# Fused attention and MLP block: low-part subtractions of the MLP on GpSimd, attention pieces at a higher rate

## The chip, the cores and the metric

The kernel runs on one core of a Trainium2 chip. The core has five engines that run side by side, each with an instruction queue of its own that is worked off in order: TensorE (PE in the profile; its weight loads are listed as PEld), VectorE (DVE), ScalarE (ACT), GpSimd (POOL) and SyncE (SP, which here issues the DMAs). They wait for each other by semaphores. The metric is the device time of one execution in microseconds (us); lower is better.

## The reference, cut to what matters

The input x has 2048 tokens of 576 channels. It is normalized, and the output is the normalized x, plus an attention, plus a token-shift mixer with an MLP behind it, plus x itself:

```python
xn = layernorm(x)
return x + A(xn, wqkv, wo) + B(xn, w1, w2, w3, w4)

# A: 32 heads of 18 channels; each token looks at 8 tokens: itself and those 2, 4, ... 14 before it
logits = q . k[pos - 2*w] * 18**-0.5;  attn = softmax(logits);  o = sum(attn * v[pos - 2*w]);  A = o @ wo
# B: shift mixer, then the MLP of 4608 hidden channels
x1 = xn + shift(gelu(layernorm(xn) @ w1)) @ w2
B = x1 + gelu(layernorm(x1) @ w3) @ w4
```

## The kernel before

Matrix products keep the precision of fp32 by splitting: each operand is the sum of a high part in the type fp32r and a low part, low = operand - high, and a product is hi*hi + hi*lo + lo*hi. So each operand has two steps of preparation: a copy into the high part on ACT (for weights `act.copy`, for the hidden values the gelu itself, once into `hi` and once into an fp32 tile `g`), and a subtraction that gives the low part. `split_w` does both for weights.

The program has stages: a projection to q, k and v (stored in DRAM as `qkvd`), the mixer with w1 and w2, then the MLP with the attention beside it, and last the product with wo. Every engine's order of work is that in which the code issues it; there is no scheduler. What the change touches is the MLP.

The MLP has 72 units (c, b): c counts 18 chunks of two blocks f of 128 hidden channels, b counts four blocks of 512 tokens. In a unit, `up` runs twice (i = 0, 1): 14 matmuls with W3 into a tile p of PSUM (two buffers), two gelus on ACT into `hi` and `g` (`g` has two buffers), and the subtraction that gives `lo` (L682). Then `down` runs four times (j = 0 to 3) for the unit before this one: 12 matmuls with W4 into a tile `ps` of PSUM (three buffers), and DVE adds `ps` to the output sums: Y += ps (L699). `split_w3` and `split_w4` prepare the weights of later blocks, one such split in most units; their raw tiles `rawf` have two buffers, loaded on SP's queue (L177, L173, L505).

The attention has no use of PE apart from the products with wqkv and wo. It is written as a Python generator of small DVE instructions ("pieces"): for each of 8 groups of 4 heads 8 products q*k (L628) and 8 reductions (L631), the scores; a softmax (L636, L641, L643, an exp on ACT, L597, L598, L600); and the weighted sum `av` with 8 products (L608) and 7 additions (L612). The weighted sum of a group comes behind the scores of the next. Loads of q, k, v and the store of the result `od` are issued on SP. In the loop over units, `bg(r)` stands ahead of each `up` and each `down`, six times in a unit, and issues pieces until their estimated cost has used up r:

```python
state["debt"] = min(state["debt"] + us, 1.5)
while state["debt"] > 0 and (late or not state["hold"]):
    cost = next(state["gen"], False)
    ...
    state["debt"] -= cost or 0.0
...
r = RATE[b] / 6 if u >= 4 else 0.0
```

The estimates are 1.3 for a piece of 1152 elements and 0.6 to 0.8 for steps of the softmax. `hold` is set before the exp and lifts only ahead of the down with j = 1. At unit 66 (z = -6) whatever is left of the attention is issued at once, its tiles give way to those of wo, and `load_o` (L738) begins to fetch its output; it is turned by 32x32 transposes on DVE (`turn`, L129 and L130), put to DRAM and fetched back (L137, L142). `split_wo` prepares wo in units 69 to 71; it calls `split_w` with DVE for the subtraction. GpSimd has little to do before the change: inverse square roots for the norms (`pow`, L89), products of one element per partition (L93) and memsets.

Of the kernel before, what the change touches and what calls it, by code (L numbers as in the profile page):

```python
# [8 lines left out]
F32 = mybir.dt.float32  # L9
F32R = mybir.dt.float32r  # L10
AF = mybir.ActivationFunctionType
ALU = mybir.AluOpType
# [33 lines left out]
def fused_block(ctx, tc, x, wqkv, wo, w1, w2, w3, w4, out):  # L46
    nc = tc.nc
    pe, act, dve, pool, sp = nc.tensor, nc.scalar, nc.vector, nc.gpsimd, nc.sync
# [108 lines left out]
    def in_order(blk):  # L157
        return blk.rearrange("p (q t c) -> p t q c", q=4, t=4)

    def by_token(blk):  # L160
        return blk.rearrange("p (t q c) -> p t q c", q=4, t=4)
# [1 line left out]
    def quads(t_, b, q):  # L163
        return dram_ap(t_, (512 * b + 128 * q) * D, [[D, 32], [32 * D, 4], [1, D]])

    def split_w(dst_hi, dst_lo, raw):
        act.copy(dst_hi, raw)  # L167
        dve.tensor_tensor(dst_lo, raw, dst_hi.bitcast(F32), op=ALU.subtract)  # L168

    def dup_tail(dst, w, col, n):  # L170
        ncols = w.shape[1]
# [66 lines left out]
    def split_cg(cg, k0, k1):  # L238
        c, n = COLS[cg]
        split_w(WQ[:, k0:k1, c:c + n], WQ[:, 5 + k0:5 + k1, c:c + n], qraw[cg][:, k0:k1, :])  # L240
# [66 lines left out]
    def split_w1(h):  # L307
        k0, k1 = (0, 3) if h == 0 else (3, 5)
        r = w1raw[h]
        for k in range(k0, k1):  # L310
            src = r[:, (k - k0) * D:(k - k0 + 1) * D].rearrange("p (g c) -> p g c", g=4)
            hi = W1[:, k, 0:512].rearrange("p (g c) -> p g c", g=4)
            lo = W1[:, 5 + k, 0:512].rearrange("p (g c) -> p g c", g=4)
            split_w(hi, lo, src[:, :, :128])
            rem = W1R[:, k, :].rearrange("p (g c) -> p g c", g=4)
            split_w(rem[:, :, 0:16], rem[:, :, 16:32], src[:, :, 128:144])
# [154 lines left out]
    for b in range(NB):  # L471
        for i, m in enumerate((0, 1, 2, 4, 3) if b < 3 else (4, 0, 1, 2, 3)):
# [12 lines left out]
            k = {(0, 4): 0, (1, 1): 1, (1, 4): 2, (2, 1): 3, (2, 4): 4}.get((b, i))  # L485
# [10 lines left out]
    raws, W3, W4 = {}, {}, {}  # L496
# [10 lines left out]
    def split_w3(f):  # L507
        if f >= NF:
            return
        t = W3[f] = wp.tile([128, 10, 128], F32R, name="W3", bufs=3)  # L510
        split_w(t[:, 0:5, :], t[:, 5:10, :], raws[f][:, :640].rearrange("p (k c) -> p k c", k=5))

    def split_w4(f):
        if f >= NF:
            return
        t = W4[f] = wp.tile([128, 2, D], F32R, name="W4", bufs=3)
        split_w(t[:, 0, :], t[:, 1, :], raws[f][:, 640:])

    x1n = {}

# [11 lines left out]
    for t in range(NT):  # L532
        ps = psb.tile([128, 2, 512], F32, name="ps", tag="b")

        def xs(a, t=t):
            if a == 4:
                return T4[:, 2 + t * 128:2 + (t + 1) * 128]
            p, g = divmod(a, 5)
            c = 2 + t * 128 - SHIFT[g]
            return H[p][g][:, c:c + 128]  # L540

        mm_tok(ps, xs, lambda b, h: W2[:, b, h * HF:(h + 1) * HF], HF)
        yv = Y[:, t, :].rearrange("p (h c) -> p h c", h=2)
        dve.tensor_tensor(yv, ps[:, :, :HF], yv, op=ALU.add)
        stats(Y[:, t, :], 2, t)
        if t in (1, 3):
            f = (t - 1) // 2
            split_w3(f)
            split_w4(f)
            load_f(f + 2)  # L550
        if 2 <= t < 6:
            n_turn(t - 2, rzpool)
        if t in (9, 10, 13, 14):
            k = {9: 4, 10: 6, 13: 8, 14: 10}[t]
            n_turn(k, rzpool)
            n_turn(k + 1, rzpool)
        if t in (8, 13):
            x1n[t // 13] = ring_block(("n", t // 13))
            get(("n", t // 13), x1n[t // 13])
        if t in (11, 15):  # L560
            split_x(x1n[t // 15])
# [110 lines left out]
    def up(c, b, i):  # L672
        f = c * C + i
        ps = psa.tile([128, 512], F32, name="p1", tag="a")
        for n, (a, w) in enumerate(PAIRS):
            pe.matmul(ps, W3[f][:, w, :], x1n[b][:, a, :], start=n == 0, stop=n == len(PAIRS) - 1)  # L676
        hi = hp.tile([128, 512], F32R, name=f"hi{i}")
        g32 = hp.tile([128, 512], F32, name="g32")
        lo = hp.tile([128, 512], F32R, name=f"lo{i}")
        act.activation(by_token(hi), in_order(ps), AF.Gelu_apprx_tanh)  # L680
        act.activation(by_token(g32), in_order(ps), AF.Gelu_apprx_tanh)  # L681
        dve.tensor_tensor(lo, g32, hi.bitcast(F32), op=ALU.subtract)  # L682
        hid[c, b, i] = (hi, lo)

    def down(c, b, j):
# [14 lines left out]

    units = [(c, b) for c in range(NCH) for b in range(NB)]
    NU = len(units)
    RATE = [6.1, 6.1, 6.1, 6.1]
    wop = None
    LATE = {(0, 0): (12, 13), (0, 1): (14, 15)}
    Wo = None
# [52 lines left out]
    for u, (c, b) in enumerate(units):  # L759
        if u == 2:  # L760
            ap_pool = apc.__enter__()
            state["gen"] = attention(ap_pool)
            next(state["gen"])
        r = RATE[b] / 6 if u >= 4 else 0.0
        z = u - NU
# [16 lines left out]
        for i in range(C):  # L782
            bg(r, False)
            up(c, b, i)
            if (u, i) in ((0, 0), (1, 0)):
                get(("n", u + 2), x1n[u + 2])
            for t in LATE.get((u, i), ()):
                n_turn(t, tp)
            if u in (1, 2) and i == 0:
                split_x(x1n[u + 1], 0)  # L790
            if z in (-4, -3) and i == 1:
                get(("o", z + 4), o_block(z + 4))
            if z == -2:
                o_turn(2, 2 * i)
                o_turn(2, 2 * i + 1)
            if z == -1:
                split_x(xo[1], i)
        if b == 3:
            split_w3(2 * c + 3)
# [14 lines left out]
        if b == 1:  # L814
            split_w3(2 * c + 2)
        if b == 2:
            split_w4(2 * c + 2)
            load_f(2 * c + 4)
        if b == 0 and c > 0:
            split_w4(2 * c + 1)  # L820
            load_f(2 * c + 3)
# [63 lines left out]
```

## Time and profile before

| | us |
|---|---|
| median of 3 runs (1300.78 to 1302.35) | 1301.79 |
| the profiled execution | 1301.86 |
| its span, first to last instruction | 1300.1 |
| PE busy | 1287.7 |
| DVE busy | 935.5 |
| ACT busy | 361.7 |
| POOL busy | 38.1 |

The MLP with the attention fills the span from about 317 to 1237 us. In the rows of the profile, `128x512` is partitions by elements per partition, a group's row has its count, its busy time, the mean length of one in ns, and the idle time of its engine ahead of it with what ended it. A row of the timeline begins with the start and the length in us. Lengths of instructions that follow each other on one engine overlap a little, so that the step from one start to the next is some 0.08 us shorter than the length. Line numbers are those of the kernel before.

### The profile page before, as it was taken

The numbers are of one execution on the slowest core, as the hardware profiler recorded it, in microseconds if no ns is written. First come the engines' busy times: TensorE is split into PE (matmuls) and PEld (weight loads), VectorE is DVE, ScalarE is ACT, GpSimd is POOL, SyncE is SP. The second block draws the span as 40 slices with busy tenths as digits, with TensorE's granted clock in tenths as the row PEclk, the third lists the DMA queues.
The fourth block names the chain that finished last, engine by engine and source line by source line (L and its number), as shares of the span: only waits on it lengthen the run. The fifth ranks groups of instructions, "written<-read, shape, count | busy, mean of one in ns | idle before, by whom it ended". The sixth has DMA issues, their size and how long they took to land.

```text
span 1300.1 us, 18507 instructions
## 1 busy us (share of the span) xinstructions
PE 1287.7 (99%) x7678; PEld 1186.9 (91%) x7678; DVE 935.5 (72%) x1336; ACT 361.7 (28%) x601; POOL 38.1 (3%) x108
## 2 busy tenths in 40 slices
PE   8999999999999999999999999999999999999898
PEld 8999998899899899999989899999999899999798
DVE  6456535778676778888878888878898877946642
ACT  3322226515422222132232232132232232122300
POOL 2011100021000000000000000000000000000000
PEclk9999999999999999999999999999999999999899
DMA  7646874345602120231221222122222102058542
GB/s 211 155 111 145 172 164 145 102 123 138 214 29 72 40 89 20 81 100 33 68 81 40 81 72 90 44 69 64 66 73 81 43 26 81 20 120 208 154 145 83
DMA packets 157828, 125.20 MB, mean 96 GB/s; under 512 B 72608, under 2 KB 129824, under 8 KB 157744
## 3 DMA queue, kind: packets, MB, share of 16 engines
q1 hardware_dynamic: 157744, 124.02, 34.4%
q8 instruction: 60, 0.98, 0.3%
q14 instruction: 24, 0.20, 0.0%
HBM read 83.56 MB, written 39.39 MB: 95 GB/s over the span
## 4 chain that ended last, share of the span: by engine, by line
PE 93%; DMA 3%; DVE 3%; SPq 1%; ACT 0%; issue 0%; POOL 0%; DVEq 0%
PE ps L696 33%; PE p L676 33%; PE ps L182 18%; PE ps L431 4%; PE ps L276 3%; DMA xd<-st 2%; DVE st L129 1%; DMA xt<-xd 1%; PE ps L446 1%; SPq L137 1%; PE ps L104 0%; DVE Y L699 0%; DMA x1n<-xd 0%; DVE bn L86 0%; PE p L853 0%
## 5 line engine op out<-in xcount | busy, mean ns | idle before, releaser
L696 PE MATMUL ps<-W,hi 128*128 128x288 f32 x2304 | 399.8, 295 | 5.2 <-DVE Y L699 5.2
L696 PEld LDWEIGHTS ps<-W,hi 128*128 128x128 f32 x2304 | 340.3, 188 | 12.1 <-DVE Y L699 5.7
L680 ACT ACTIVATE hi<-p 128x512 fp32r<-128x512 f32 x144 | 86.2, 598 | 576.1 <-PE p L676 576.1
L696 PE MATMUL ps<-W,lo 128*128 128x288 f32 x1152 | 245.8, 295 | 0.0
L676 PE MATMUL p<-x1n,W 128*128 128x512 f32 x1008 | 236.0, 391 | 0.0
L676 PE MATMUL p<-xt,W 128*128 128x512 f32 x1008 | 234.5, 389 | 0.0
L676 PEld LDWEIGHTS p<-x1n,W 128*128 128x128 f32 x1008 | 188.4, 189 | 37.2
L699 DVE TENSOR_TENSOR Y<-ps,Y 128x576 f32<-128x576 f32 x288 | 212.1, 749 | 13.5 <-PE ps L696 13.5
L676 PEld LDWEIGHTS p<-xt,W 128*128 128x128 f32 x1008 | 187.3, 188 | 36.9
L682 DVE TENSOR_TENSOR lo<-g,hi 128x512 fp32r<-128x512 f32 x144 | 99.4, 691 | 158.1 <-ACT g L681 158.0
L696 PEld LDWEIGHTS ps<-W,lo 128*128 128x128 f32 x1152 | 185.9, 188 | 0.0
L182 PE MATMUL ps<-WQ,xt 128*128 128x432 f32 x672 | 134.4, 359 | 0.0
L182 PEld LDWEIGHTS ps<-WQ,xt 128*128 128x128 f32 x672 | 125.5, 188 | 5.4
L628 DVE TENSOR_TENSOR prod<-q,k 128x1152 f32<-128x1152 f32 x64 | 86.4, 1350 | 0.0
L631 DVE TENSOR_REDUCE L<-prod 128x64 f32<-128x1152 f32 x64 | 86.2, 1347 | 0.0
L681 ACT ACTIVATE g<-p 128x512 f32<-128x512 f32 x144 | 85.3, 592 | 0.0
L612 DVE TENSOR_TENSOR o<-o,prod 128x1152 f32<-128x1152 f32 x56 | 75.6, 1350 | 0.0
L608 DVE TENSOR_TENSOR prod<-v,L 128x1152 f32<-128x1152 f32 x56 | 75.6, 1350 | 0.0
L167 ACT CAST W<-rawf 128x640 fp32r<-128x640 f32 x72 | 50.3, 700 | 70.5 <-PE ps L696 69.2
L168 DVE TENSOR_TENSOR W<-rawf,W 128x640 fp32r<-128x640 f32 x72 | 56.3, 785 | 0.0
L182 PE MATMUL ps<-W,h 128*128 128x288 f32 x384 | 53.5, 295 | 0.0
L182 PEld LDWEIGHTS ps<-W,h 128*128 128x128 f32 x384 | 51.9, 188 | 0.1
(108 smaller groups left out, 888.2 us busy)
## 6 DMA issues: line engine op xcount, KB each, us to landing
xd<-st SPq DMA_DIRECT2D x48, 320.0 KB, 6.0
qkvd<-stg SPq DMA_DIRECT2D x24, 432.0 KB, 3.5
rawf<-in_B_w_dram SPq DMA_DIRECT2D x36, 288.0 KB, 3.1
rawf<-in_B_w_dram SPq DMA_DIRECT2D x36, 256.0 KB, 2.9
xt<-xd SPq DMA_DIRECT2D x8, 768.0 KB, 5.1
xin<-in_A_x_dram SPq DMA_DIRECT2D x16, 288.0 KB, 3.8
q<-qkvd SPq DMA_DIRECT2D x8, 576.0 KB, 3.9
k<-qkvd SPq DMA_DIRECT2D x8, 576.0 KB, 5.6
```

Source lines behind the costliest of these rows:

```text
L168: dve.tensor_tensor(dst_lo, raw, dst_hi.bitcast(F32), op=ALU.subtract)
L182: pe.matmul(ps[:, h, :n], xs(a), ws(b, h), start=i == 0, stop=i == len(PAIRS) - 1)
L608: dve.tensor_tensor(dst, vv, Lf[:, :, w:w + 1].to_broadcast([128, TPP * GH, HD]), op=ALU.mult)
L612: dve.tensor_tensor(o, o, dst, op=ALU.add)
L628: dve.tensor_tensor(prod.rearrange("p (j h) d -> p j (h d)", h=GH), q, k[:, r0:r0 + TPP, :], op=ALU.mult)
L631: dve.tensor_reduce(Lf[:, :, w], prod, axis=AX.X, op=ALU.add)
L676: pe.matmul(ps, W3[f][:, w, :], x1n[b][:, a, :], start=n == 0, stop=n == len(PAIRS) - 1)
L680: act.activation(by_token(hi), in_order(ps), AF.Gelu_apprx_tanh)
L681: act.activation(by_token(g32), in_order(ps), AF.Gelu_apprx_tanh)
L682: dve.tensor_tensor(lo, g32, hi.bitcast(F32), op=ALU.subtract)
L696: pe.matmul(ps[:, k, :HF], h[:, col], w[:, p, k * HF:(k + 1) * HF], start=n == 0, stop=n == len(seq) - 1)
L699: dve.tensor_tensor(yv, ps[:, :, :HF], yv, op=ALU.add)
```

## The change

Three subtractions move from DVE's queue to POOL's: the one of `lo` in `up`, and those in `split_w3` and `split_w4`. The copies and gelus on ACT stay. `RATE` goes from 6.1 to 8.6, so a call of `bg` hands out pieces of up to 1.43 us in place of 1.02. The subtractions for wo, wqkv, w1 and w2 stay on DVE.

```diff
-    def split_w(dst_hi, dst_lo, raw):
+    def split_w(dst_hi, dst_lo, raw, eng=dve):
         act.copy(dst_hi, raw)
-        dve.tensor_tensor(dst_lo, raw, dst_hi.bitcast(F32), op=ALU.subtract)
+        eng.tensor_tensor(dst_lo, raw, dst_hi.bitcast(F32), op=ALU.subtract)
...
-        split_w(t[:, 0:5, :], t[:, 5:10, :], raws[f][:, :640].rearrange("p (k c) -> p k c", k=5))
+        split_w(t[:, 0:5, :], t[:, 5:10, :], raws[f][:, :640].rearrange("p (k c) -> p k c", k=5), pool)
...
-        split_w(t[:, 0, :], t[:, 1, :], raws[f][:, 640:])
+        split_w(t[:, 0, :], t[:, 1, :], raws[f][:, 640:], pool)
...
-        dve.tensor_tensor(lo, g32, hi.bitcast(F32), op=ALU.subtract)
+        pool.tensor_tensor(lo, g32, hi.bitcast(F32), op=ALU.subtract)
...
-    RATE = [6.1, 6.1, 6.1, 6.1]
+    RATE = [8.6, 8.6, 8.6, 8.6]
```

How the queues change shows at three places. The first is DVE in a weighted sum. Before, this is unit 22, one of the full ones (`W_5497` is a W3, `lo` the low part of a hidden tile):

```order
L168 TENSOR_TENSOR W_5497<-rawf,W_5497 128x640
L612 TENSOR_TENSOR o<-o,prod 128x1152
L682 TENSOR_TENSOR lo_5518<-g_5517,hi_5516 128x512
L608 TENSOR_TENSOR prod<-v,L 128x1152
L682 TENSOR_TENSOR lo_5541<-g_5540,hi_5539 128x512
L612 TENSOR_TENSOR o<-o,prod 128x1152
L699 TENSOR_TENSOR Y<-ps,Y 128x576 x2
L608 TENSOR_TENSOR prod<-v,L 128x1152
L699 TENSOR_TENSOR Y<-ps,Y 128x576
L612 TENSOR_TENSOR o<-o,prod 128x1152
L699 TENSOR_TENSOR Y<-ps,Y 128x576
```

After, a full unit of a weighted sum (unit 16) stands thus on DVE:

```order
L612 TENSOR_TENSOR o<-o,prod 128x1152
L608 TENSOR_TENSOR prod<-v,L 128x1152
L612 TENSOR_TENSOR o<-o,prod 128x1152
L608 TENSOR_TENSOR prod<-v,L 128x1152
L699 TENSOR_TENSOR Y<-ps,Y 128x576
L612 TENSOR_TENSOR o<-o,prod 128x1152
L699 TENSOR_TENSOR Y<-ps,Y 128x576
L608 TENSOR_TENSOR prod<-v,L 128x1152
L699 TENSOR_TENSOR Y<-ps,Y 128x576
L612 TENSOR_TENSOR o<-o,prod 128x1152
L699 TENSOR_TENSOR Y<-ps,Y 128x576
```

Five pieces have become seven, one stands ahead of nearly every sum, and the three subtractions are gone.

The second place is POOL in the same part of the program. Before, POOL's queue ends with the memsets of the attention's mask, ahead of unit 2:

```order
L93 TENSOR_TENSOR rs_81<-mv_78,rs_81 128x1
L578 MEMSET mask 128x512
L580 MEMSET mask 1x8
L580 MEMSET mask 1x16
L580 MEMSET mask 1x24
```

After, it goes on through the whole MLP, here for three units:

```order
L682 TENSOR_TENSOR lo_5349<-g_5348,hi_5347 128x512
L682 TENSOR_TENSOR lo_5371<-g_5370,hi_5369 128x512
L168 TENSOR_TENSOR W_5448<-rawf,W_5448 128x576
L682 TENSOR_TENSOR lo_5476<-g_5475,hi_5474 128x512
L682 TENSOR_TENSOR lo_5499<-g_5498,hi_5497 128x512
L168 TENSOR_TENSOR W_5566<-rawf,W_5566 128x640
L682 TENSOR_TENSOR lo_5588<-g_5587,hi_5586 128x512
L682 TENSOR_TENSOR lo_5610<-g_5609,hi_5608 128x512
```

Each unit has two subtractions for hidden tiles and one for weights there now.

The third place is DVE in unit 70, where wo is prepared and the attention's output `ot` is turned. Before:

```order
L168 TENSOR_TENSOR Wo<-rawf,Wo 128x1152
L682 TENSOR_TENSOR lo_10945<-g_10944,hi_10943 128x512
L129 STREAM_TRANSPOSE st<-ot 128x16x32
L130 STREAM_TRANSPOSE st<-ot 128x4x32
L129 STREAM_TRANSPOSE st<-ot 128x16x32
L130 STREAM_TRANSPOSE st<-ot 128x4x32
L682 TENSOR_TENSOR lo_10970<-g_10969,hi_10968 128x512
L129 STREAM_TRANSPOSE st<-ot 128x16x32
L130 STREAM_TRANSPOSE st<-ot 128x4x32
L129 STREAM_TRANSPOSE st<-ot 128x16x32
L130 STREAM_TRANSPOSE st<-ot 128x4x32
L699 TENSOR_TENSOR Y<-ps,Y 128x576 x4
```

After:

```order
L168 TENSOR_TENSOR Wo<-rawf,Wo 128x1152
L129 STREAM_TRANSPOSE st<-ot 128x16x32
L130 STREAM_TRANSPOSE st<-ot 128x4x32
L129 STREAM_TRANSPOSE st<-ot 128x16x32
L130 STREAM_TRANSPOSE st<-ot 128x4x32
L129 STREAM_TRANSPOSE st<-ot 128x16x32
L130 STREAM_TRANSPOSE st<-ot 128x4x32
L129 STREAM_TRANSPOSE st<-ot 128x16x32
L130 STREAM_TRANSPOSE st<-ot 128x4x32
L699 TENSOR_TENSOR Y<-ps,Y 128x576 x4
```

The two subtractions that stood ahead of the four sums are gone; the rest is unchanged. The last piece of the attention, in unit 65 before, stands in unit 47 after.

## Prediction

> **What bounds the kernel now.** I read the head of the page first, then the busy time by stretch, then who waits for whom, then the groups, and last the timeline at the places where TensorE (PE) stands still.
>
> ```profile
> span 1300.1 us, 18507 instructions
> PE 1287.7 (99%) x7678; PEld 1186.9 (91%) x7678; DVE 935.5 (72%) x1336; ACT 361.7 (28%) x601; POOL 38.1 (3%) x108
> ...
> PEclk9999999999999999999999999999999999999899
> ```
>
> ```profile
> 700.00:750.00 50.00, 50.00 (x300) 45.54 (x299) 42.72 (x48) 11.14 (x20) 0.00 (x0) 1.00 0.22 66
> ...
> 1200.00:1250.00 50.00, 45.42 (x289) 42.93 (x288) 28.71 (x45) 14.24 (x22) 0.00 (x0) 0.93 0.64 173
> ```
>
> ```profile
> PE ps L696 <- DVE Y L699: 5.2, 2, 4.6
> ```
>
> The columns of a stretch are its length, then the busy time of PE, PE's weight loads, DVE (VectorE), ACT (ScalarE) and POOL (GpSimd), the granted clock, DMA share and rate. In the MLP, PE is busy 50.00 of 50 us with DVE at 42.72, 85%: DVE's work is hidden whole, and taking some away saves nothing there by itself. PE's waits for DVE are two, 5.2 us in all, one of 4.6; that one lies in the stretch from 1200, where the clock falls to 0.93 as well. So there is little to win and much that can be lost: DVE's spare time is what the higher rate spends.
>
> **The price of a subtraction on POOL.** By shape, the groups that leave DVE and the nearest rows of POOL:
>
> ```profile
> L682 DVE TENSOR_TENSOR lo<-g,hi 128x512 fp32r<-128x512 f32 x144 | 99.4, 691 | 158.1 <-ACT g L681 158.0
> ...
> L168 DVE TENSOR_TENSOR W<-rawf,W 128x640 fp32r<-128x640 f32 x36 | 29.6, 821 | 0.0
> L168 DVE TENSOR_TENSOR W<-rawf,W 128x576 fp32r<-128x576 f32 x36 | 26.9, 748 | 0.0
> ```
>
> ```profile
> L93 POOL TENSOR_TENSOR rs<-mv,rs 128x1 f32<-128x1 f32 x16 | 3.1, 195 | 1.3
> ...
> L405 POOL MEMSET h<- 128x2 f32 x8 | 0.6, 100 | 23.4 <-PE ps L182 22.8 <-issue 0.5
> ...
> L578 POOL MEMSET mask<- 128x512 f32 x1 | 0.5, 527 | 0.0
> ```
>
> No large subtraction on POOL is in this trace. A memset of 512 elements takes 0.53 us against 0.10 for two, so one pass over 512 costs 0.43 us; a subtraction of one element costs 0.195. From below, everything overlaps in one pass: 0.53 us. From above, two reads and a write in turn: 0.195 + 3 x 0.43 = 1.49. With two reads in turn and the write beside them it is 1.05; I take the middle of 1.05 and 1.49, 1.27 us, of which 1.08 is work on the elements, and by length 1.54 us for 640 and 1.41 for 576. A unit of the MLP has two such for the gelu and one for weights, some 4.0 us of POOL in 12.7. POOL is idle else, so its own queue keeps up.
>
> Page "GPSIMD Engine Reference" of the Trainium skill, section "Elementwise — side-by-side cycle accounting", gives 4497 ns for 2048 elements; with the 0.195 of the row above that is an estimate of 1.27 us for 512, and no run here shows it.
>
> **Does POOL get in DVE's way?** Here the timeline answers for one direction. The first row is a small power on POOL with nothing in its way, the rest is one place where DVE subtracts two SBUF tensors:
>
> ```profile
> 262.33 0.55 POOL L89 TENSOR_TENSOR rs<-rs,mhalf 128x1 f32<-128x1 f32 x1 [65.95 <-DVE mv L92]
> ...
> 264.29 1.50 DVE L168 TENSOR_TENSOR W<-rawf,W 128x640 fp32r<-128x640 f32 x2
> 264.34 1.18 POOL L89 TENSOR_TENSOR rs<-rs,mhalf 128x1 f32<-128x1 f32 x1 [1.20 <-DVE mv L92]
> ...
> 265.70 0.75 DVE L544 TENSOR_TENSOR Y<-ps,Y 128x576 f32<-128x576 f32 x1
> ```
>
> The power takes 1.18 us in place of 0.55: it ends at 265.52, 0.41 behind the end of DVE's first subtraction (264.29 + 0.82 = 265.11). So POOL's read waits until DVE's two-input instruction is through. Whether DVE waits as long for a long read on POOL is not in the trace: DVE's second subtraction ran in its usual 0.75, but a read of one element holds nothing. Ends: no hold at all, 0 us, and a hold for the whole 1.08 us each time. I take the hold, since one side of it is visible, but only where DVE's next instruction also has two SBUF inputs; the sums Y += ps have one (ps lies in PSUM) and the reductions one.
>
> Page "SBUF — State Buffer" of the Trainium skill, section "Who interferes with whom", says that a DVE instruction with two SBUF inputs contends with a GpSimd instruction that reads SBUF, and that the first holds the shared pair for its whole instruction. The trace agrees for POOL behind DVE (1.18 against 0.55 us); against "the whole instruction" stands that the second subtraction wasn't late though the power ran until 265.52. By the page's word each hold would be 1.27 rather than 1.08 us, and the sum below some 4 us more (0.2 x 2 per unit over half of 44 units, half forgiven).
>
> **DVE's load in the attention.** Pieces and sums step as follows, and a unit is the distance of two PE rows:
>
> ```profile
> 609.30 1.35 DVE L612 TENSOR_TENSOR o<-o,prod 128x1152 f32<-128x1152 f32 x1
> ...
> 610.57 0.75 DVE L699 TENSOR_TENSOR Y<-ps,Y 128x576 f32<-128x576 f32 x1
> ...
> 611.24 1.35 DVE L608 TENSOR_TENSOR prod<-v,L 128x1152 f32<-128x1152 f32 x1
> ```
>
> ```profile
> 1172.71 6.52 PE L676 MATMUL p<-xt,W 128*128 128x512 f32 x28
> 1179.07 0.69 PE L696 MATMUL ps<-W,hi 128*128 128x288 f32 x4
> ...
> 1185.41 4.93 PE L676 MATMUL p<-xt,W 128*128 128x512 f32 x21
> ```
>
> ```profile
> L628 DVE TENSOR_TENSOR prod<-q,k 128x1152 f32<-128x1152 f32 x64 | 86.4, 1350 | 0.0
> L631 DVE TENSOR_REDUCE L<-prod 128x64 f32<-128x1152 f32 x64 | 86.2, 1347 | 0.0
> ...
> L612 DVE TENSOR_TENSOR o<-o,prod 128x1152 f32<-128x1152 f32 x56 | 75.6, 1350 | 0.0
> L608 DVE TENSOR_TENSOR prod<-v,L 128x1152 f32<-128x1152 f32 x56 | 75.6, 1350 | 0.0
> ...
> L643 DVE TENSOR_TENSOR L<-L,mx 128x512 f32<-128x512 f32 x8 | 5.5, 688 | 0.1
> ...
> L598 DVE RECIPROCAL mx<-mx 128x64 f32<-128x64 f32 x8 | 4.4, 553 | 0.3
> ```
>
> A piece costs DVE 1.27 us, a sum 0.67, each of the six steps of a softmax 0.5 to 0.6; a unit is 12.70 us, 6.36 of ups and four downs of 1.58. Before, a full unit has 5 pieces, 4 sums, 2 gelu subtractions and one or two of weights: 6.35 + 2.68 + 2 x 0.61 + 0.7 = 10.95 us, or 12.3 with two weights and one add of x. After, a full unit has 7 pieces and 4 sums: 8.89 + 2.68 = 11.57, with the add of x 12.2. Without any hold that fits, as 12.3 did. The subtractions removed are worth 0 on PE, since PE was full above them; the attention's last piece moves from unit 65 to unit 47, and is worth 0 too, because the first load of its output (L738) stands at unit 66 in both programs.
>
> With holds: in the weighted sum (av) all seven pieces have two SBUF inputs. The first gelu subtraction falls among the pieces of the ups, hold 1.08. The second and that of the weights (608/512 x 1.08 = 1.28) fall among the downs, where a sum of 0.67 stands between two pieces and runs beside POOL: 0.41 and 0.61. Together 2.1 us, so 13.7 us in 12.70: DVE falls 1.0 behind per unit. In the scores (L628, L631) every second piece is a reduction of 1.27, longer than the hold; I put about 1 us there, and 11.57 + 1 fits. A dense stretch of a group is the unit with the softmax (two pieces of scores and two of the weighted sum 5.1, softmax 3.5, sums and add 3.35, so 12.0; + 1.5) and two units of the weighted sum (11.57 + 2.1): overruns 0.8, 1.0 and 1.0, 2.8 us. PE stands only once the ring of three ps is full: the fourth down (6.36 + 3 x 1.58 = 11.1 into the unit) needs the first sum, ready at 6.36 + 1.58 = 7.9 and done 0.75 later, so 2.4 us of lateness is forgiven, of which the unit's own first hold takes 1.1. That leaves 2.8 - 1.3 = 1.5 us of PE in such a stretch; where the softmax falls into a lighter unit it is nearer 0.5. I take 1 us for each of 8 groups, 8 us. From below 0 (no hold); from above nothing hides behind sums and reductions: 2 x 1.08 + 1.28 = 3.4 us, 15.0 in 12.70, 2.3 us over 16 units that are nearly all weighted sum, 37 us.
>
> **The end of the MLP.** The one long stall, read on ACT, DVE and PE:
>
> ```profile
> 1206.34 1.16 ACT L167 CAST Wo<-rawf 128x1152 fp32r<-128x1152 f32 x1 [8.59 <-DMA rawf<-in_A_wo_dram]
> ```
>
> ```profile
> 1173.43 0.72 DVE L699 TENSOR_TENSOR Y<-ps,Y 128x576 f32<-128x576 f32 x1
> ...
> 1207.53 1.36 DVE L168 TENSOR_TENSOR Wo<-rawf,Wo 128x1152 fp32r<-128x1152 f32 x1 [6.27 <-ACT Wo L167]
> 1208.81 0.68 DVE L682 TENSOR_TENSOR lo<-g,hi 128x512 fp32r<-128x512 f32 x1
> 1209.41 0.70 DVE L129 STREAM_TRANSPOSE st<-ot 128x512 f32<-128x512 f32 x1
> ...
> 1213.19 2.05 DVE L699 TENSOR_TENSOR Y<-ps,Y 128x576 f32<-128x576 f32 x3
> ```
>
> ```profile
> 331.46 0.80 PE L696 MATMUL ps<-W,hi 128*128 128x288 f32 x4 [0.60 <-DVE Y L699]
> ...
> 1172.45 0.43 PE L696 MATMUL ps<-W,lo 128*128 128x288 f32 x2
> ...
> 1213.97 1.33 PE L696 MATMUL ps<-W,hi 128*128 128x288 f32 x4 [4.58 <-DVE Y L699]
> ```
>
> DVE waits 6.27 us for the DMA of Wo by way of ACT, then works off Wo, two gelu subtractions and four turns before the first sum that PE needs. The two subtractions (0.6 each on this path) go: -1.2. Three units earlier DVE reaches the last sum at 1173.43, though PE was done at 1172.88; without subtractions ahead of it, it is 0.5 earlier, and so are the turn behind it, the DMAs that chain from it and Wo: -0.5. The wait of 0.60 at 331 stands behind the same kind of subtractions: -0.6. Together -2.3; the stall falls from 4.6 to 2.9 us. The clock is the open part:
>
> ```profile
> 1214.00:1217.00 3.00, 3.00 (x12) 3.00 (x13) 1.24 (x2) 0.00 (x0) 0.00 (x0) 0.50 0.87 168
> ```
>
> Behind the stall PE runs at 0.50. Ups of 6.3 and a down of 1.58 from 1213.97 would put the next down at 1221.8; it came at 1224.5, so the slow clock costs 2.7 us. I keep it in the sum, as the only row there is.
>
> Page "TensorE: Matmul & The Clock Gate" of the Trainium skill, section "Part 1: The HAM clock gate", puts the slow clock behind an idle window of about 3.4 us. The trace agrees with 4.6 us being long enough; a gap of 2.9 would spare the 2.7 us, and the sum would be 1305 in place of 1308.
>
> **What else is moved, at 0.** PE needs lo a unit later, some 6 us of ups and more away, against 1.3 to 3 us on POOL. ACT's second gelu needs g two uses back, 6.4 us earlier. The weight loads on SP wait for POOL where they waited for DVE, with q, k and v behind them; ACT still casts first, and POOL is at most a hold late. Near unit 0 POOL's powers queue behind 2.95 us of weights, with n_turn two tiles later as cover.
>
> **Sum.** 1301.86 (the profiled execution; the median of the runs, 1301.79, is the same) - 2.3 + 8 = 1307.6, so 1308.
>
> **Rivals.** (a) DVE is not held, or POOL's work is nearer 0.5 us: the attention fits, and only the end is left, 1299.5, or 1297 if the clock stays up there. For it: the second subtraction was not late. Against: POOL was. (b) Holds without cover or a slower POOL: up to +37, 1320 to 1337. For it: 184 of 248 pieces (64 + 56 + 64 against 64 reductions) have two SBUF inputs; against: sums and reductions between. It decides from 1.1 us of hold per unit, DVE's spare time at 11.57. (c) The clock rule with my holds: 1305.
>
> **Chances.** Held in part (1302 to 1320, with (c)): 0.46. (a): 0.36, of it 0.2 with the clock up. (b): 0.18. A measurement here tells about 0.2%, 2.6 us. Faster is (a) with the clock up and a sliver more, 0.23; same is the rest of (a) and the lowest part of the forecast, 0.2; slower 0.57. The range 1297 to 1330 leaves out the upper half of (b) and little of (a).
>
> **What would show it.** Sums Y late behind pieces whose time is above 1.35 us while POOL subtracts; PE's waits on Y in units 11 to 46, 1 to 2 us each, at the fourth down; none in units 48 to 65. POOL's lo above 1.27 us mean, drawn out by its own waits. The stall near 1210 shorter by 1.7 us. If pieces keep 1.35 us beside POOL, the hold is wrong and (a) holds; if POOL's lo is under 0.8 us, its price is.

## The result, and the profile after

| | before | after |
|---|---|---|
| median of 3 runs, us | 1301.79 | 1330.89 (1328.43 to 1331.9) |
| ratio | | 1.0222 [1.0208, 1.0236] |
| span of the profiled execution, us | 1300.1 | 1326.7 |

The change made the kernel 29 us slower, 2.2%. The forecast was 1308, with a range of 1297 to 1330: the direction was right, but the loss of 29 us was nearly five times the 6 us that were forecast, and the time lies just above the range. The profiled execution is the fastest of the three (1328.43 us); the others ran at a lower mean granted clock (0.990 and 0.994 against 0.995).

The head of the page after (span, busy times, DVE by slices, shares of the chain that ended last):

```profile
span 1326.7 us, 18662 instructions
PE 1294.0 (98%) x7678; PEld 1191.0 (90%) x7678; DVE 869.2 (66%) x1120; ACT 362.0 (27%) x601; POOL 388.3 (29%) x324
...
DVE  6456525777488799999799999978622222224642
...
PE 62%; DVE 31%; DMA 4%; issue 1%; SPq 1%; ACT 1%; ACTq 0%; DVEq 0%
```

DVE's total fell from 935.5 to 869.2 us, and yet DVE now holds 31% of the chain (3% before). The slices tell why: nines through the first part of the MLP and twos behind it. The work got less in sum and too dense in one place.

Who waits for whom, as before:

```profile
PEld ps L696 <- DVE Y L699: 29.5, 17, 3.9
PE ps L696 <- DVE Y L699: 25.4, 15, 3.7
```

Fifteen waits of PE for sums instead of two. Now the groups (shape, count, busy us, mean ns); the pieces were 1347 to 1350 ns before, and `lo` and `W` were DVE's:

```profile
L682 POOL TENSOR_TENSOR lo<-g,hi 128x512 fp32r<-128x512 f32 x144 | 215.0, 1494 | 517.9 <-ACT g L681 516.0 <-DMA ot<-od 1.9
...
L628 DVE TENSOR_TENSOR prod<-q,k 128x1152 f32<-128x1152 f32 x64 | 102.9, 1608 | 0.8
L608 DVE TENSOR_TENSOR prod<-v,L 128x1152 f32<-128x1152 f32 x56 | 94.7, 1690 | 0.7
L612 DVE TENSOR_TENSOR o<-o,prod 128x1152 f32<-128x1152 f32 x56 | 93.5, 1670 | 0.8
L631 DVE TENSOR_REDUCE L<-prod 128x64 f32<-128x1152 f32 x64 | 86.2, 1347 | 1.0
L168 POOL TENSOR_TENSOR W<-rawf,W 128x640 fp32r<-128x640 f32 x36 | 68.9, 1913 | 0.2 <-ACT W L167 0.2
```

The three large groups of pieces with two SBUF inputs are drawn out by 0.26 to 0.34 us in the mean, (258 x 64 + 340 x 56 + 320 x 56) ns = 53.5 us in all. The reduction with one input (L631) keeps its 1347 ns. POOL's subtractions are drawn out as well.

Four stretches: unit 10 (units are counted as in the prediction, the first is 0), where DVE waits with the exp held back, units 11 and 12, and all of units 11 to 24:

```profile
435.25:447.95 12.70, 12.70 (x79) 11.60 (x77) 5.38 (x7) 5.94 (x8) 4.44 (x3) 1.00 0.02 6
447.95:463.23 15.28, 12.96 (x78) 11.63 (x77) 15.21 (x13) 2.79 (x5) 5.22 (x3) 1.00 0.15 42
463.23:477.08 13.85, 12.95 (x78) 11.63 (x77) 13.75 (x12) 2.77 (x5) 4.44 (x2) 1.00 0.00 0
447.95:635.95 188.00, 179.57 (x1066) 162.61 (x1065) 186.56 (x163) 45.45 (x76) 74.88 (x41) 1.00 0.24 74
```

The columns are those of the prediction's stretches: length, then PE, weight loads, DVE, ACT and POOL busy, granted clock, DMA. In units 11 and 12 DVE is busy for 15.21 of 15.28 and 13.75 of 13.85 us, and a unit is as long as DVE's work in it. Fourteen units that take 177.8 us of PE take 188.0, with DVE at 99%.

### The profile page after: what moved, and what is told of

It reads as the page before. It is cut to its first block, busy times and chain, and to the rows that moved or that the text cites. A ratio compares the mean times of both kernels' runs of the same rounds, so it can differ in the third digit from the quotient of the medians.

```text
span 1326.7 us, 18662 instructions
## 1 busy us (share of the span) xinstructions
PE 1294.0 (98%) x7678; PEld 1191.0 (90%) x7678; DVE 869.2 (66%) x1120; ACT 362.0 (27%) x601; POOL 388.3 (29%) x324
## 4 chain that ended last, share of the span: by engine, by line
PE 62%; DVE 31%; DMA 4%; issue 1%; SPq 1%; ACT 1%; ACTq 0%; DVEq 0%
PE ps L182 18%; PE p L676 18%; PE ps L696 18%; DVE prod L608 6%; DVE o L612 6%; DVE Y L699 6%; DVE prod L628 5%; PE ps L431 4%; DVE L L631 3%; PE ps L276 3%; DMA xd<-st 1%; DVE o L608 1%; DVE st L129 1%; DMA k<-qkvd 1%; SPq L137 1%
## 5 line engine op out<-in xcount | busy, mean ns | idle before, releaser
L699 DVE TENSOR_TENSOR Y<-ps,Y 128x576 f32<-128x576 f32 x288 | 214.9, 749 | 245.4 <-PE ps L696 245.3
L682 POOL TENSOR_TENSOR lo<-g,hi 128x512 fp32r<-128x512 f32 x144 | 215.0, 1494 | 517.9 <-ACT g L681 516.0
L168 POOL TENSOR_TENSOR W<-rawf,W 128x640 fp32r<-128x640 f32 x72 | 138.4, 1923 | 72.7 <-ACT W L167 72.7
L628 DVE TENSOR_TENSOR prod<-q,k 128x1152 f32<-128x1152 f32 x64 | 102.9, 1608 | 0.8
L89 POOL TENSOR_TENSOR rs<-rs,mhalf 128x1 f32<-128x1 f32 x48 | 29.8, 621 | 249.7 <-DVE rs L88 148.5
L608 DVE TENSOR_TENSOR prod<-v,L 128x1152 f32<-128x1152 f32 x56 | 94.7, 1690 | 0.7
L612 DVE TENSOR_TENSOR o<-o,prod 128x1152 f32<-128x1152 f32 x56 | 93.5, 1670 | 0.8
L631 DVE TENSOR_REDUCE L<-prod 128x64 f32<-128x1152 f32 x64 | 86.2, 1347 | 1.0
L182 PE MATMUL ps<-W,h 128*128 128x288 f32 x384 | 53.5, 295 | 0.0
```

Source lines behind the costliest of these rows:

```text
L168: eng.tensor_tensor(dst_lo, raw, dst_hi.bitcast(F32), op=ALU.subtract)
L182: pe.matmul(ps[:, h, :n], xs(a), ws(b, h), start=i == 0, stop=i == len(PAIRS) - 1)
L608: dve.tensor_tensor(dst, vv, Lf[:, :, w:w + 1].to_broadcast([128, TPP * GH, HD]), op=ALU.mult)
L612: dve.tensor_tensor(o, o, dst, op=ALU.add)
L628: dve.tensor_tensor(prod.rearrange("p (j h) d -> p j (h d)", h=GH), q, k[:, r0:r0 + TPP, :], op=ALU.mult)
L631: dve.tensor_reduce(Lf[:, :, w], prod, axis=AX.X, op=ALU.add)
```

## The experiments

There were three theories: H, DVE is overfilled, by a rate that leaves no room for holds; R, the rate makes the loss by itself; and P, POOL's own length or queue makes something late.

**The parts, one at a time.** First the subtractions alone, at the old rate:

```diff
-    RATE = [8.6, 8.6, 8.6, 8.6]
+    RATE = [6.1, 6.1, 6.1, 6.1]
```

> The subtractions on GpSimd as in the changed kernel, the rate back at 6.1. Theory H (holds on a full DVE): a full unit of weighted sum has 5 pieces, 6.35 + 2.68 us, and with the 2.4 us of holds per such unit that the changed kernel's trace shows it is 11.4 of 12.7, so PE never waits; the end of the MLP keeps the gain of 4 us that the changed kernel has there: 1297.5 us (1296 to 1299). Theory P (GpSimd's slowness itself reaches PE or ACT, through lo or the weights): the loss stays, over 1315 us. Theory R (the rate alone is the loss) also expects 1297.5 here; the next kernel tells it from H.

1297.68 us (1295.74 to 1299.83), ratio 0.9964 [0.9951, 0.9976]: 0.4% faster than before. Only the waits at the start and at the end of the MLP are left:

```profile
PE 1287.1 (99%) x7678; PEld 1187.2 (91%) x7678; DVE 835.9 (64%) x1120; ACT 362.0 (28%) x601; POOL 382.9 (30%) x324
...
PE ps L696 <- DVE Y L699: 4.0, 2, 3.4
```

POOL does the same subtractions here as in the changed kernel, so P falls; H and R both expected this. Then the rate alone, on the kernel before:

```diff
-    RATE = [6.1, 6.1, 6.1, 6.1]
+    RATE = [8.6, 8.6, 8.6, 8.6]
```

> The kernel before with the rate at 8.6 and nothing else; all subtractions on DVE. Theory R: the rate alone makes the loss, so 1330 us or more. Theory H: no holds, but the subtractions are DVE's again: over the dense run of units 11 to 24 the order gives 13.2 us a unit for 12.7, 7 us per 16 units less about 2 forgiven, three such runs and a little for the slow clock, no gain at the end: 1318 us (1310 to 1326). If the rate cost nothing it would be 1302.

1329.41 us (1327.81 to 1331.22), ratio 1.0208 [1.0194, 1.0221]. By its number this is R, which expected 1330 or more; H had expected 1318 (1310 to 1326) and was wrong on the size. With the subtractions on DVE the rate alone costs as much as the whole change:

```profile
PE 1297.7 (98%) x7678; PEld 1192.5 (90%) x7678; DVE 937.1 (70%) x1336; ACT 362.2 (27%) x601; POOL 38.2 (3%) x108
...
PE ps L696 <- DVE Y L699: 24.6, 17, 4.8
...
447.50:635.00 187.50, 180.17 (x1055) 162.67 (x1054) 184.49 (x201) 45.66 (x76) 0.00 (x0) 0.99 0.24 74
```

In nearly the same stretch DVE is busy for 184.49 of 187.50 us without a hold, and for 186.56 of 188.00 with POOL at work. At the high rate, moving the subtractions to POOL gave DVE back nothing there. R and H differ in what they expect once neither the subtractions nor the holds are there, and that is the next run.

**The reads taken away.** Each subtraction on POOL becomes three memsets of its output, which write three times and read nothing; the low parts are left out of the result:

```diff
-        pool.tensor_tensor(lo, g32, hi.bitcast(F32), op=ALU.subtract)
+        for _ in range(3):
+            pool.memset(lo.bitcast(F32), 0.0)
```

(and the same in `split_w` where it runs on POOL)

> The changed kernel with each subtraction on GpSimd replaced by three memsets of the same low part (the low parts are zero, so those terms of the products are left out): GpSimd is busy for at least as long (3 x 0.53 us for 512 elements against 1.27) and writes more, but reads nothing. Theory H with the read as its cause: the pieces fall back to 1.35 us, PE doesn't wait in units 8 to 47, 1297 us (1295 to 1300). Rival: GpSimd's writes hold DVE as well, then pieces stay drawn out and it takes 1315 us or more.

1298.6 us (1296.98 to 1299.12), ratio 0.9969 [0.9958, 0.998]. POOL is as busy as in the changed kernel (387.2 us); the pieces are back at their old length (L632 and L612 here are L628 and L608):

```profile
L632 DVE TENSOR_TENSOR prod<-q,k 128x1152 f32<-128x1152 f32 x64 | 86.6, 1352 | 0.8
L612 DVE TENSOR_TENSOR prod<-v,L 128x1152 f32<-128x1152 f32 x56 | 75.7, 1352 | 0.7
```

So POOL's writes do not hold DVE. What this run takes away is the reads (and the arithmetic that goes with them), and at rate 8.6 the holds are worth 32 us. R is wrong: with DVE free of both the subtractions and the holds the rate costs nothing, and the prediction's 11.57 us of work per unit do fit into 12.7. In units 11 to 24 (446.51 to 624.31 us here, 449.55 to 638.48 in e2) DVE is busy for 164.0 us in this run, 186.0 with the subtractions on DVE and 186.6 in the changed kernel: some 22 us of subtractions came off DVE, and as much in holds came in their place.

**Does lateness carry from unit to unit, or does one unit lose by itself?** The scores are slowed, so that DVE catches up ahead of each weighted sum:

```diff
-                    yield 1.3
+                    yield 1.75
```

(at both pieces of the scores)

> The changed kernel with the estimate of a piece of the scores raised from 1.3 to 1.75, so that scores come at 5 pieces a unit and weighted sums at 6 to 7 as in the changed kernel: DVE starts each weighted sum on time. Theory C (lateness is carried from stretch to stretch through the scores, which at 8.6 give nothing back): most of the 31 us in the attention go, 0.5 to 1 us per group stay: 1304 us (1299 to 1309). Theory S (a weighted sum by itself costs 3.9 us of PE, whatever comes ahead of it): 1325 us (1318 to 1331).

1335.6 us (1332.37 to 1338.15), ratio 1.0253 [1.0234, 1.0272]. Carrying alone is refuted: DVE stands idle for 2.8 to 4.1 us in most units of the scores, and yet PE waits 2.7 to 3.7 us at each weighted sum. The time is above both ranges, that of theory S (1318 to 1331) too. The timeline shows the place:

```profile
477.65 2.50 POOL L682 TENSOR_TENSOR lo<-g,hi 128x512 fp32r<-128x512 f32 x1 [1.81 <-ACT g L681]
...
479.03 2.34 DVE L612 TENSOR_TENSOR o<-o,prod 128x1152 f32<-128x1152 f32 x1
...
480.83 1.68 POOL L682 TENSOR_TENSOR lo<-g,hi 128x512 fp32r<-128x512 f32 x1 [0.68 <-ACT g L681]
481.40 2.32 DVE L608 TENSOR_TENSOR prod<-v,L 128x1152 f32<-128x1152 f32 x1
...
482.47 2.65 POOL L168 TENSOR_TENSOR W<-rawf,W 128x640 fp32r<-128x640 f32 x1
...
483.75 2.58 DVE L612 TENSOR_TENSOR o<-o,prod 128x1152 f32<-128x1152 f32 x1
486.26 0.74 DVE L699 TENSOR_TENSOR Y<-ps,Y 128x576 f32<-128x576 f32 x1
...
487.06 1.33 PE L696 MATMUL ps<-W,hi 128*128 128x288 f32 x4 [2.68 <-DVE Y L699]
```

Three pieces in a row are held, one for each of POOL's subtractions, by 1.0, 1.0 and 1.2 us, all ahead of the unit's first sum. If that row of holds is what costs, a first sum that comes one piece earlier must help. One call of `bg` is moved from between the ups to ahead of the third down, in this kernel and in the changed one:

```diff
-            bg(r, False)
+            if i == 0:
+                bg(r, False)
...
                 bg(r, j == 1)
                 down(*prev, j)
...
+                if j == 2:
+                    bg(r, False)
```

> The kernel e4 (the changed kernel with a scores' piece counted as 1.75 us, 1335.6 us) with one of the pieces between the two ups handed out ahead of the third down instead: as many pieces in a unit, and the first sum of a unit reached a piece and a hold (some 2.5 us) earlier on DVE. Theory clump (the loss comes where three held pieces in a row stand ahead of the first sum): the first sum is then late by less than the 2.4 us that the ring of ps forgives, most of the loss goes, 1300 to 1310 us, and PE's waits on Y fall from some 16 to a few. Theory throughput (DVE simply has more work, with holds, than a unit has time): the order within the unit changes nothing, 1328 to 1336 us.

> The changed kernel (1330.9 us) with the same shift of one piece from between the ups to ahead of the third down. Theory clump: 1300 to 1312 us. Theory throughput: 1325 to 1333 us, since DVE is busy without a gap in the stretch of units 11 to 24 already, with pieces of 1.6 to 1.9 us in place of 1.35. I lean to throughput for the dense stretch and to clump for the rest: 1320 us.

With the slow scores 1322.98 us (1317.78 to 1323.56), ratio 1.0151 [1.0129, 1.0174]: 12.6 of the 34 us that e4 had lost come back, fewer than the clump theory wanted. Two held pieces still stand ahead of the sum:

```profile
559.37 2.33 DVE L608 TENSOR_TENSOR prod<-v,L 128x1152 f32<-128x1152 f32 x1
...
561.74 2.58 DVE L612 TENSOR_TENSOR o<-o,prod 128x1152 f32<-128x1152 f32 x1
564.24 0.74 DVE L699 TENSOR_TENSOR Y<-ps,Y 128x576 f32<-128x576 f32 x1
```

With the change as it is, 1331.56 us (1327.25 to 1332.98), ratio 1.0221 [1.0198, 1.0243]: nothing comes back. My lean, 1320, was a miss, and the time is that of the throughput theory. The trace does not make throughput the only reason: DVE is busy for 179.68 us in the same fourteen units, 1.9 more than the 177.8 that PE needs, and they last 190.95. Most of DVE's idle time there is one wait of 7.2 us at 590 us, with the exp held back. The fourteen units:

```profile
447.56:638.51 190.95, 182.47 (x1066) 165.46 (x1065) 179.68 (x157) 45.42 (x76) 72.24 (x41) 0.98 0.23 73
```

**Where it tips.** The changed kernel at rate 7.3:

```diff
-    RATE = [8.6, 8.6, 8.6, 8.6]
+    RATE = [7.3, 7.3, 7.3, 7.3]
```

> The changed kernel with rate 7.3 in place of 8.6 (6.1 gave 1297.7 us, 8.6 gives 1330.9). DVE in a unit of the weighted sum: 6 pieces x 1.27 + four sums 2.68 + half an add of x 0.3 + holds 2.4 = 13.0 us in 12.7, against 14.3 at seven pieces and 11.7 at five. If a unit loses what its DVE has over 12.7 (throughput), some 20 units lose 0.3 us: 1297.7 + 6 = 1304 us, with the loss only where two full units follow each other. If the loss goes with the rate in proportion, 1297.7 + 33 x 1.2/2.5 = 1313 us. If a threshold only at seven pieces counts, 1298 us.

1299.28 us (1297.44 to 1300.45), ratio 0.9976 [0.9964, 0.9988]. Nearly all the loss lies between 7.3 and 8.6: it is a threshold, not a slope. The pieces are held for 55.7 us in all, as much as at 8.6, but DVE is busy for only 158.9 of 178.0 us in units 11 to 24. In PE's waits there are two new ones, at 967 and 980 us (0.78 and 0.26), and the old one at the end of the MLP:

```profile
PE ps L696 <- DVE Y L699: 4.3, 3, 3.2
```

**Holds doubled at the low rate**, on the version e8 below:

```diff
         pool.tensor_tensor(lo, g32, hi.bitcast(F32), op=ALU.subtract)
+        pool.tensor_tensor(lo, g32, hi.bitcast(F32), op=ALU.subtract)
```

> e8 with the gelu's subtraction issued twice on POOL (the same values written again), so that the holds on DVE double and the number of DVE's instructions stays as in e8. If held time is what fills DVE: a unit of the weighted sum has 6.35 + 2.68 + 0.3 + 2.4 + 2 = 13.7 us at the low rate, as much as at rate 8.6 with single holds, over some 20 units: 1303 to 1315 us, with PE's waits on Y back. If the pieces handed out per unit decide and holds are small change: 1293 to 1295 us.

1294.59 us (1294.23 to 1295.03), against 1293.01 without the doubling. This was a miss, and a useful one:

```profile
L608 DVE TENSOR_TENSOR prod<-v,L 128x1152 f32<-128x1152 f32 x56 | 105.7, 1887 | 0.5
L628 DVE TENSOR_TENSOR prod<-q,k 128x1152 f32<-128x1152 f32 x64 | 104.2, 1628 | 0.5
L612 DVE TENSOR_TENSOR o<-o,prod 128x1152 f32<-128x1152 f32 x56 | 103.0, 1839 | 0.4
...
447.59:625.83 178.24, 178.13 (x1066) 162.33 (x1065) 145.92 (x132) 45.43 (x76) 116.33 (x69) 1.00 0.22 68
```

The pieces are held for (537 x 56 + 278 x 64 + 489 x 56) ns = 75 us, more than the 53.5 of the changed kernel and the 26 of e8, and the time grows by only 1.6 us. DVE is busy for 146 of 178 us in these units. Held time costs next to nothing as long as the units have room for it. My expectation had counted five pieces per unit everywhere; the rate hands out 6.1/1.3 = 4.7, and the softmax takes part of that.

**Half of the move.** The changed kernel with the gelu's subtractions back on DVE and those of W3 and W4 on POOL:

```diff
-        pool.tensor_tensor(lo, g32, hi.bitcast(F32), op=ALU.subtract)
+        dve.tensor_tensor(lo, g32, hi.bitcast(F32), op=ALU.subtract)
```

> The changed kernel (rate 8.6) with the gelu's subtractions back on DVE and only those of W3 and W4 on POOL. DVE takes back 2 x 0.61 = 1.2 us a unit and loses two holds of 1.0. If a subtraction on POOL costs DVE as much in holds as it saves, the time stays with that of the rate alone and of the whole change: 1327 to 1333 us. If holds are what makes the whole change lose: 1318 to 1323. If moving the gelu's subtractions is a net gain in spite of the holds: 1335 or more.

1329.16 us (1328.19 to 1330.38), ratio 1.0208 [1.0193, 1.0224]. At rate 8.6 none of the subtractions, those of the weights and all of them on POOL give 1329.4, 1329.2 and 1330.9 us. In units 11 to 24 DVE is busy for 186.6 of 188.05 us here: with DVE full of two-input pieces, POOL's help is taken back in holds. At rate 6.1 the same move did relieve DVE, from 149.6 us in these units before to 132.1 in e1.

**A better version.** In e1 the one long stall is at the end of the MLP: ACT and DVE stand waiting for Wo's DMA with a gelu and sums queued behind them. The second and third piece of Wo are cast and split behind the downs:

```diff
-        if z == -2:
-            split_wo(2)
-            load_wo(4)
-        if z == -1:
-            split_wo(4)
+        if z == -2:
+            load_wo(4)
...
+            if z in (-2, -1):
+                split_wo({-2: 2, -1: 4}[z])
```

> The changed kernel at rate 6.1 (1297.7 us) with the second and third piece of Wo cast and split behind the downs of their unit instead of ahead of its ups, so that ACT and DVE do not stand waiting for that DMA with a gelu and sums queued behind them. If the wait at the end of the MLP (3.4 us and the slow clock behind it) came from that order alone, it goes: 3.4 + some 1.5 for the clock, 1293 us. If the chain of turns, stores and loads on SP's queue behind it sets the end anyway (the loads of xo come later for another reason), PE waits as long at the next place: 1296 to 1298 us.

> The kernel before (subtractions on DVE, rate 6.1) with the second and third piece of Wo cast and split behind the downs, as in e8. If the order at the end gave all that e8 gained over e1, this one gains as much over before: the unit of 18.9 us becomes 12.7, 1301.8 - 6.2 = 1295.6 us, and POOL's subtractions are worth 2 to 3 us at the start only. If DVE, which still has two gelu subtractions per unit, is late there, the wait stays in part: 1297 to 1300.

> e8 again, beside e9 on the same chip and with more rounds: 1292.7 us within 1. The difference to e9 is what POOL's subtractions are worth in the best version: 2 to 4 us.

At rate 6.1 with POOL 1292.67 us (1292.48 to 1292.96), ratio 0.9928 [0.9912, 0.9943]; again, beside the next one, 1293.01 (1292.89 to 1293.04), 0.9931 [0.9919, 0.9944]. The kernel before with this edit alone gives 1294.08 (1294.04 to 1295.6), 0.9944 [0.9932, 0.9957]. No wait of PE for a sum is left in the profile of e8, and DVE is at 132 of 178 us in the stretch used above:

```profile
PE 1283.2 (99%) x7678; PEld 1184.3 (92%) x7678; DVE 835.9 (65%) x1120; ACT 362.1 (28%) x601; POOL 382.9 (30%) x324
...
447.59:625.83 178.24, 178.24 (x1067) 162.78 (x1066) 132.38 (x132) 45.52 (x76) 67.56 (x42) 1.00 0.21 66
```

This is the best version, and its gain is not the change's: of 8.6 us against before, 7.6 come from the order at the end and 1.1 from POOL, where I had expected 2 to 4. That fits the start of the MLP: the trace of e9 has two waits of PE there, 0.42 us at 331 and 1.41 at 346, and that of e8 has none.

## Why the prediction was wrong in size, step by step

**The price on POOL: right.** Taken as 1.27 us for 512 elements; the shortest `lo` took 1.27 us and the median one 1.29. The mean of 1494 has POOL's own waits in it, as the prediction's last paragraph said it would. For 576 elements the estimate was 1.41 and the shortest took 1.43; for 640 it was 1.54 and 1.56. The Trainium skill's page "GPSIMD Engine Reference", section "Elementwise — side-by-side cycle accounting", gave the same 1.27 as an estimate from its 4497 ns for 2048 elements, and the trace agrees.

**The hold: right, in kind, direction and sum.** Taken as 1.08 us on pieces with two SBUF inputs; the timeline of e4 has 1.0, 1.0 and 1.2 us, that of unit 11, shown further down, 1.1 and 1.25, the reduction and the sums are untouched, and in e3 the holds go with the reads. The prediction's terms make 16 x 2.1 + 8 x 1.5 + 16 x 1 = 62 us of holds in the attention; the three groups above show 53.5, and the first product of each group (8 of 1859 ns, 1358 before) and a step of the softmax (8 of 1061 ns, 688 before) another 7.

**The conversion into PE's time: the step that failed.** The prediction put overruns of 0.8, 1.0 and 1.0 us on a group, took 1.3 us off as forgiven by the ring of `ps`, and rounded the rest to 1 us for each of 8 groups, 8 us. In units 11 to 46 PE lost 31 us, 3.9 for each group. By the prediction's own overruns, forgiven once for each of the three stretches named below, 8 x 2.8 - 3 x 1.3 = 18.5 us would have been left, near the 21.8 that PE's waits there add to; the other 9 us come after the waits, and the prediction had no term for them. Three things were wrong in it:

- *The work in the units.* A unit with the softmax was put at 13.5 us and one of the weighted sum at 13.7; in units 11 and 12 DVE was busy for 15.2 and 13.75. The end of the softmax and a held product stood at the end of unit 10, ahead of three of its sums; these fell into unit 11, beside six pieces, an add of x and two sums of its own.
- *The forgiveness.* 2.4 us less one hold assumed a DVE that is on time when a unit begins, and a single hold ahead of the first sum. In units 11 and 12 DVE worked 28.96 us and PE lost 29.13 - 25.40 = 3.7 us: of the 3.6 us of overrun nothing was forgiven. The timeline of unit 11 shows two full holds, of the second `lo` and of the weights, ahead of the first sum; the prediction had put both among the downs, behind sums, at 0.41 and 0.61:

```profile
455.67 1.29 POOL L682 TENSOR_TENSOR lo<-g,hi 128x512 fp32r<-128x512 f32 x1 [1.88 <-ACT g L681]
455.71 2.47 DVE L612 TENSOR_TENSOR o<-o,prod 128x1152 f32<-128x1152 f32 x1
...
456.92 2.68 POOL L168 TENSOR_TENSOR W<-rawf,W 128x640 fp32r<-128x640 f32 x1
...
458.21 2.60 DVE L608 TENSOR_TENSOR prod<-v,L 128x1152 f32<-128x1152 f32 x1
...
460.74 0.74 DVE L699 TENSOR_TENSOR Y<-ps,Y 128x576 f32<-128x576 f32 x1
461.40 1.34 DVE L612 TENSOR_TENSOR o<-o,prod 128x1152 f32<-128x1152 f32 x1
461.53 0.67 PE L696 MATMUL ps<-W,hi 128*128 128x288 f32 x3 [2.31 <-DVE Y L699]
```

- *Once per group.* DVE has no gap of more than 0.2 us in a unit from unit 11 to 24, so lateness that one group leaves is there for the next. Its long rests in units 10 to 46 are three, 7.2 us each at 443, 657 and 872 us, each where an exp is held back. That makes three stretches, and lateness can be forgiven once in each, not eight times.

One wait has something else in it, the longest:

```profile
DVE o L608 <- DMA v<-qkvd: 3.7, 1, 3.7
...
920.96 1.33 PE L696 MATMUL ps<-W,hi 128*128 128x288 f32 x4 [3.70 <-DVE Y L699]
```

The weighted sum of the last group follows directly on the one before, and its `v` is loaded only behind that one, so DVE stands 3.7 us for the DMA in unit 45, which takes 18.0 us. The prediction had put the loads at 0. In e3 DVE waits 3.9 us for the same load, and its unit takes 12.8: the wait cost PE only where DVE was full.

How the 31 us split: the waits of PE in these units add to 21.8 us; a unit in which the clock stays up is some 0.3 us longer than its wait (15.28 - 12.70 = 2.6 against 2.31 in unit 11); and behind four of the waits PE ran at a slow clock, which made those units another 1.3 us longer (some 5 us). How much of the waits is carried lateness and how much the order within a unit stays open: with gaps between the groups the order was worth 12.6 us (e4 to e5), in the changed kernel nothing in sum (e6).

**The end of the MLP: right on the stall, and lucky on the clock.** The stall was to shrink by 1.7 us (4.6 to 2.9):

```profile
1237.58 0.69 PE L696 MATMUL ps<-W,hi 128*128 128x288 f32 x4
...
1238.03 1.36 DVE L168 TENSOR_TENSOR Wo<-rawf,Wo 128x1152 fp32r<-128x1152 f32 x1 [6.04 <-ACT Wo L167]
...
1242.49 2.05 DVE L699 TENSOR_TENSOR Y<-ps,Y 128x576 f32<-128x576 f32 x3
1243.26 0.80 PE L696 MATMUL ps<-W,hi 128*128 128x288 f32 x4 [3.14 <-DVE Y L699]
```

It is 3.14, and its unit 16.1 us where it was 18.9. The sum had kept the slow clock there; it did not come, as the Trainium skill's page "TensorE: Matmul & The Clock Gate", section "Part 1: The HAM clock gate", would have it for a gap of less than 3.4 us. That was luck: at the same place the clock was 0.50 behind a wait of 2.93 us in e5 and of 3.23 us in e7. From this unit to the end the changed kernel is 4.1 us shorter, against 1.7 without and 4.4 with that rule. The wait of 0.60 near 331 went, but one of 0.48 came at 344.7; that wait and the stall together were -2.3 in the sum.

**The moved loads and POOL's queue at 0: right at rate 6.1**, where e1 has no other wait; at 8.6 the last load of `v` is the exception named above. **The rivals.** The time is that of (b), "holds without cover", 1320 to 1337, with a chance of 0.18, but only in part by its mechanism: the holds sum to what the forecast had (in units 11 and 12 they are 3.0 and 2.0 us, against its 2.1 and (b)'s 3.4), and what was missing is the forgiveness. (b)'s test was the right one: it decides from 1.1 us of hold per unit, and the 53.5 us of three groups are 1.2 per unit over 44 units, by more in the weighted sums. The prediction had this threshold and a forecast above it, and then let a cushion take the difference away. It also valued the rate's part as harmless ("without any hold that fits"), which e3 bears out, and gave the subtractions' removal no weight; e2 and e3 show that they and the holds are worth some 30 us each, one in place of the other.

## What to carry to other kernels

Work moved from DVE to POOL helped here only while DVE had room: where DVE is full of instructions that read two SBUF tensors, what POOL takes over comes back as holds, so count the moved work as still on DVE before you spend the room. Sum the helper engine's load by unit, with what is late from the unit before, against the unit's length; beyond the threshold expect the whole overrun on the bound engine, and subtract a buffer's slack once per stretch and not once per group. And look at the profile's single long stall first: an order changed by two lines there was worth seven times what POOL's help was.

## What the runs showed of the hardware

The hold goes both ways. DVE's piece of 1.35 us took 2.3 to 2.6 us beside one of POOL's subtractions, and POOL's subtraction of 640 elements up to 2.69 us where its shortest took 1.56. POOL's writes alone held nothing (1352 ns beside three memsets in e3).

The slow clock did not follow the length of PE's wait alone. Three stretches behind a wait (length, busy times, then the granted clock, third from the end), and the row of the second wait; those of the other two stand above:

```profile
461.60:464.60 3.00, 3.00 (x19) 2.77 (x20) 3.00 (x3) 0.00 (x0) 0.00 (x0) 1.00 0.03 5
675.00:678.00 3.00, 3.00 (x13) 3.00 (x14) 3.00 (x3) 0.00 (x0) 0.00 (x0) 0.50 0.00 0
1244.10:1247.10 3.00, 3.00 (x18) 2.65 (x17) 1.86 (x3) 0.00 (x0) 0.00 (x0) 1.00 0.92 174
```

```profile
674.94 1.33 PE L696 MATMUL ps<-W,hi 128*128 128x288 f32 x4 [2.31 <-DVE Y L699]
```

Behind 2.31 us at 461.5 the clock stayed at 1.00, behind 2.31 us at 674.9 it was 0.50, and behind 3.14 us at 1243.3 it was 1.00. The page "TensorE: Matmul & The Clock Gate" of the Trainium skill, cited above, puts the slow clock behind an idle window of about 3.4 us; the measurement decides, and a wait of 2.3 us can be enough. What else decides was not found.
